# Gated linear attention with an MLP on one core: a new chunk order, uncast loads, and one queue for nearly every load

## The chip, the cores and the metric

The kernel runs on one core of a Trainium2 chip. The metric is the device time of one execution in microseconds (us). The fast executions of one kernel lie within 1.5% of each other here, often within 0.5%; an execution that is over 1.5% above the fastest of its kernel counts as slow and is left out of ratios. Times quoted for a kernel are medians over its runs. A ratio is computed as the mean time of one kernel's fast runs over the mean time of the other's fast runs of the same rounds on the same chip, so it is not quite the ratio of the medians that are quoted beside it. Experiments ran on several chips, so an experiment is judged by its ratio to the kernel before in its own rounds.

## The reference, cut to what matters

```python
# q, k, v, alpha: (B=4, H=8, S=768, D=48) float32
state = zeros((B, H, D, D))
for t in range(S):
    state = alpha[:, :, t, :, None] * state + einsum('bhd,bhe->bhde', k[:, :, t], v[:, :, t])
    y[:, :, t] = einsum('bhd,bhde->bhe', q[:, :, t], state)
x = y.transpose(0, 2, 1, 3).reshape(B * S, H * D)      # 3072 tokens x 384
h = maximum(x @ w_in, 0.0)                             # w_in 384 x 2048
out = (h * h) @ w_out                                  # w_out 2048 x 384
```

The recurrence carries a state from token to token within a batch. The four batches don't depend on each other.

## The kernel before

The kernel handles the sequence in 24 chunks of 128 tokens, six for each batch. Within a chunk it works with matrices: it takes the logarithm of alpha (L_s), sums it along the tokens with a matmul, forms A = exp(sum) and Ainv = exp(-sum), multiplies q by A and k by Ainv (qA and kI), transposes them, computes masked scores (sm), and adds the part that comes from the state of the chunk before (sb). The state (st) advances once in a chunk. The chunk's output, transposed into xT_big, is the input of the MLP. The MLP's matmuls need far more of TensorE than the recurrence, and a built-in planner weaves the two together.

It is a list scheduler that runs when the kernel is built. Every piece of work is an `Op` with an engine, an assumed duration and dependencies; the planner simulates the engines with those durations, and the kernel then emits every instruction in the planned order, which each engine keeps. If an assumed duration is wrong, the emitted program stays correct.

```python
class Plan:
    ...
    def run(self, gate):
        ...                      # picks, over all engines, the op that can start first (then by prio)
            op.start = t + getattr(op, "late", 0.0)
            free[eng] = t + op.dur
        ...
        self.order.sort(key=lambda o: o.start)     # instructions are emitted in this order
```

In the kernel before, the first four chunks of batch 0 are handled together. For these, alpha and q are loaded so that one partition takes four consecutive tokens. One descriptor row is then 4 x 48 floats, 768 bytes. All other q, k, v and alpha tiles have one token on a partition, so a row is 48 floats, 192 bytes. k and, later, alpha and q are issued by SyncE (seven of these transfers by GpSimd); v is cast to bf16 in its transfer, which GpSimd issues; the weights too are cast in their transfers by GpSimd.

```python
slot_srcs = {n: a[0, :, 0:4 * P, :].rearrange("h (p j) d -> p h (j d)", j=4) for n, a in srcs}  # 768-byte rows
srcs = [(n, a.rearrange("b h (c p) d -> b c p h d", p=P)) for n, a in srcs]                    # 192-byte rows
...
def pool_dma(dur, issue, emit, *deps):          # a transfer that GpSimd issues, in order
    i = add("POOL", issue, emit, *deps, *w_gate, prio=-50.0, lat=0.0, at=4.6)
    w_gate[:] = [i]
    return add("DMA", dur, lambda: None, i, lat=2.0)
...
def load_tile(nm):
    if nm == "vt":
        return loads.tile([P, H, D], BF16, name=nm, bufs=LBV)     # v: cast in the transfer
    return loads.tile([P, H, D], FP32, name=nm)
...
ld_at = [load_slots("at", i * H // 2, (i + 1) * H // 2) for i in range(2)]   # SyncE, 384 KB each
ld_qt = [load_slots("qt", i * H // 2, (i + 1) * H // 2) for i in range(2)]
for s in range(NJ):
    add_loads(s, ("kt", "vt"), pool=s == NJ - 1)
four_slots(ld_at, ld_qt)
...
for x in "iiiioo4oo5":                          # i, o: quarters of w_in, w_out (384 KB); 4, 5: a chunk's loads
    ...
```

Of the kernel before, what the change touches and what calls it, by code (L numbers as in the profile page):

```python
# [110 lines left out]
def kernel(  # L111
# [24 lines left out]
    slot_srcs = {n: a[0, :, 0:4 * P, :].rearrange("h (p j) d -> p h (j d)", j=4) for n, a in srcs}  # L136
    srcs = [(n, a.rearrange("b h (c p) d -> b c p h d", p=P)) for n, a in srcs]
# [7 lines left out]
    LBV = 6  # L145
# [10 lines left out]
    NJ = 4  # L156
    PQ = P // NJ
# [4 lines left out]
    kI_s = big.tile([P, NBUF, H, DP], BF16)  # L162
    ae_s = big.tile([P, NBUF, NP, 2], FP32)
    nc.vector.memset(warm, 0.0)
    for t in (L_s, qA_s, kI_s):
        nc.vector.memset(t[:, :, :, D:], 0.0)
    nc.vector.memset(ae_s, 0.0)
# [4 lines left out]

    t_lag = consts.tile([P, NJ, P], FP32)
    first_t = consts.tile([P, 1], FP32)
    mk4 = consts.tile([P, NJ, P], BF16)
    for c in range(NJ):
        nc.vector.memset(first_t[c * PQ:(c + 1) * PQ], -float(c * P))
    nc.gpsimd.iota(t_lag, pattern=[[-1, NJ], [1, P]], base=0, channel_multiplier=-NJ,
                   allow_small_or_imprecise_dtypes=True)
    nc.vector.tensor_scalar(mk4, t_lag, first_t, None, op0=ALU.is_ge)  # L180


    def within(out, cols, step=1):

        for base, sgn in ((0, 1), (PQ - 1, -1)):
            nc.gpsimd.affine_select(out=out, in_=out, compare_op=ALU.is_ge, fill=0.0,
                                    base=base, pattern=[[-PQ * sgn, NJ]] + cols, channel_multiplier=sgn)
    mq_incl = consts.tile([P, P], BF16)
    mq_strict = consts.tile([P, P], BF16)
    nc.gpsimd.memset(mq_incl, 1.0)  # L190
    within(mq_incl.rearrange("p (c u) -> p c u", c=NJ), [[0, PQ]])
    for out, base in ((mq_strict, -1), (mq_incl, 0)):
        nc.gpsimd.affine_select(out=out, in_=mq_incl, compare_op=ALU.is_ge, fill=0.0,
                                base=base, pattern=[[1, P]], channel_multiplier=-1)
    ones_blk = consts.tile([P, NJ], BF16)
    nc.gpsimd.memset(ones_blk, 1.0)
    within(ones_blk, [])

    def causal(out, pattern):
        nc.gpsimd.memset(out, 1.0)  # L200
        nc.gpsimd.affine_select(out=out, in_=out, compare_op=ALU.is_ge, fill=0.0,
                                base=0, pattern=pattern, channel_multiplier=-1)
    utri_p = consts.tile([P, 1, P], BF16)
    causal(utri_p[:, 0, :].rearrange("p (j t) -> p j t", j=NJ), [[1, NJ], [NJ, PQ]])
    ident_bf = consts.tile([P, P], BF16)
    make_identity(nc, ident_bf)
    utri_b = consts.tile([P, 1, P], BF16)
    causal(utri_b[:, 0, :], [[1, P]])
    ones_col = consts.tile([P, 1], BF16)
    nc.gpsimd.memset(ones_col, 1.0)  # L210
    slot = {n: big.tile([P, H, NJ, D], FP32, name=f"slot_{n}") for n in ("at", "qt")}
    qT4 = big.tile([P, NP, NJ, NJ, PQ], BF16)
    xT_big = big.tile([P, KT, n_tok], BF16)
    ident_by_token = ident_bf.rearrange("p (j t) -> p t j", j=NJ)
# [13 lines left out]
    def tr(*a):  # L228
# [4 lines left out]
        "sm0": -56.473, "cpq1": -50.279, "ps3": -49.423, "tq0": -43.954, "qA3": -43.948, "ln1": -42.551,  # L233
        "sb1": -40.005, "stm2": -40.004, "stm1": -40.000, "sb2": -40.000, "sb3": -40.000, "p13": -39.839,
        "kI1": -38.583, "p30": -36.979, "sb0": -36.132, "xT3": -35.894, "p31": -33.712, "sm1": -32.534,
        "pk": -31.000, "A0": -30.000, "pq0": -30.000, "qA0": -29.999, "Ai2": -29.995, "xn2": -29.992, "qA1":
        -29.899, "A1": -29.899, "pq1": -29.899, "qA2": -29.800, "pq2": -29.799, "xn1": -29.792, "A3":
        -29.700, "ps1": -28.550, "xn0": -27.270, "tq2": -22.798, "tq1": -22.219, "tq3": -20.369, "Ai0":
        -20.000, "A2": -19.910, "cp3": -19.910, "pq3": -19.909, "Ai1": -19.900, "Ai3": -19.699, "stm3":
        -19.005, "cpq2": -19.003, "pae": -19.000, "ae0": -18.999, "ln0": -17.727, "cp1": -17.717, "stm0":  # L240
        -17.111, "p10": -10.000, "cp0": -10.000, "kI0": -9.999, "p40": -9.999, "p21": -9.993, "p41": -9.989,
        "p32": -9.986, "p20": -9.984, "kI2": -9.980, "cp2": -9.980, "p11": -9.980, "ps2": -9.979, "p12":
        -9.979, "p43": -9.979, "p33": -9.970, "xn3": -9.970, "sm3": -9.970, "kI3": -9.969, "p23": -9.969,
        "p42": -9.960, "ps0": -9.272, "xT0": -9.000, "xT2": -9.000, "xT1": -9.000, "p22": -8.991, "ae1":
        -7.468, "cpq3": -6.554, "sm2": -6.554, "cpq0": -3.046,
# [15 lines left out]
    LD = 0.97  # L261
    WLD = 2.1
# [14 lines left out]
    X_ISSUE = 0.9  # L277
    w_gate = []

    def pool_dma(dur, issue, emit, *deps):  # L280

        i = add("POOL", issue, emit, *deps, *w_gate, prio=-50.0, lat=0.0, at=4.6)
        w_gate[:] = [i]
        return add("DMA", dur, lambda: None, i, lat=2.0)
# [16 lines left out]
    def hold_x(d, before, nm):  # L301
        def e_hold():
            d["at"] = loads.tile([P, H, D], FP32, name="at")
            pin(nc.gpsimd.tensor_copy(d["at"][:, 0, 0:1], before[nm][:, 0, 0:1]))
        d["go"] = add("POOL", 0.1, e_hold, before["ld_" + nm], prio=-6.0)

    PAIRS = 10
    C = [dict() for _ in range(NT)]
    state = {}
    made = {nm: [] for nm, _ in srcs}  # L310

    def load_tile(nm):
        if nm == "vt":
            return loads.tile([P, H, D], BF16, name=nm, bufs=LBV)
        return loads.tile([P, H, D], FP32, name=nm)

    def load_slots(nm, lo, hi):
        def ld():
            pin(nc.sync.dma_start(out=slot[nm][:, lo:hi].rearrange("p h j d -> p h (j d)"),  # L319
                                  in_=slot_srcs[nm][:, lo:hi]))  # L320
        return add("DMA", 2.5 * (hi - lo) / H, ld, lat=2.0, at=0.9)

    def add_loads(s, names=("at", "qt", "kt", "vt"), pool=False, after=None):
        d = C[s]
        b, c = divmod(s, NCH)
        for nm, src in srcs:
            if nm not in names:
                continue
            m = made[nm]
            n = LBV if nm == "vt" else LB  # L330
            prev = C[m[-n]]["use_" + nm] if len(m) >= n else None
            m.append(s)

            def ld(nm=nm, src=src):
                if nm not in d:
                    d[nm] = load_tile(nm)
                if nm == "vt" and after:
                    pin(nc.gpsimd.tensor_copy(d[nm][:, 0, 0:1], after["kt"][:, 0, 0:1]))  # L338
                pin((nc.gpsimd if pool or nm == "vt" else nc.sync).dma_start(out=d[nm], in_=src[b, c]))  # L339
# [514 lines left out]
```

## Time and profile before

| what | before | view |
|---|---|---|
| median of 3 runs | 192.5 us (191.35 to 194.46) | times |
| span of the profiled execution | 189.4 us | page |
| TensorE busy | 180.2 us, 95% | page |
| first w_in matmul | 22.50 us | chain of waits |
| quarters of w_in landed | 17.86, 20.34, 22.25, 24.15 us | GpSimd's waits |
| TensorE's granted clock | half from about 17.9 to 24.7 us | windows |

These lines are from the page of the kernel before: the span, the busy time of each engine, TensorE's granted clock in tenths and the transfer rate in 40 slices of the span, and the two DMA queues (packets, MB, share). PE is TensorE, POOL is GpSimd; q1 is the queue that SyncE issues to, q0 is GpSimd's.

```profile
span 189.4 us, 5215 instructions
...
PE 180.2 (95%) x1999; PEld 137.1 (72%) x1999; DVE 132.3 (70%) x335; ACT 126.7 (67%) x346; POOL 42.2 (22%) x78
...
PEclk9998589999999999999999999999999999999999
...
GB/s 177 238 165 203 204 223 211 125 183 147 183 191 185 206 180 173 201 153 188 218 130 142 166 84 124 170 87 126 0 45 43 3 42 45 6 37 45 42 42 83
...
q1 hardware_dynamic: 64992, 17.45, 44.8%
q0 software_dynamic: 29120, 6.88, 37.5%
```

TensorE is the bound for nearly the whole span. What can still be won lies in the first 22 us. The chain of waits that ended last (start us, length us, what) says what this start is made of:

```profile
6.33 9.01 DMA kt<-in_k_dram
...
22.50 15.27 PE bank L226 x139
...
167.36 18.95 PE bank L226 x152
```

A wait of 9 us for a k tile, then the state chain of the first chunks, and from 22.50 us on TensorE. The last of these lines is the final block of 152 matmuls.

The windows of the kernel before (window; busy us and instructions of PE, PEld, DVE, ACT, POOL; granted clock; DMA share; GB/s):

```profile
4.00:6.00 2.00, 1.54 (x13) 0.84 (x12) 0.00 (x0) 1.54 (x2) 1.99 (x5) 1.00 1.01 279
...
8.00:10.00 2.00, 2.00 (x22) 1.23 (x21) 0.57 (x2) 2.00 (x6) 2.00 (x4) 1.00 2.05 163
...
12.00:14.00 2.00, 1.23 (x20) 0.97 (x20) 1.23 (x3) 1.26 (x4) 0.77 (x1) 1.00 1.63 162
...
20.00:22.00 2.00, 2.00 (x25) 1.38 (x25) 1.73 (x4) 1.34 (x4) 0.88 (x1) 0.50 1.25 205
...
25.00:26.50 1.50, 1.50 (x22) 1.14 (x20) 0.51 (x2) 1.17 (x3) 0.38 (x1) 1.00 1.27 278
...
28.00:32.50 4.50, 4.50 (x44) 4.03 (x42) 2.95 (x8) 3.77 (x7) 2.66 (x3) 1.00 1.49 194
...
40.00:42.00 2.00, 2.00 (x25) 1.35 (x24) 1.29 (x2) 0.17 (x1) 0.00 (x0) 1.00 1.60 177
```

The last column is about 163 where k tiles in 192-byte rows and cast v tiles load together from the two queues (a cast tile counts with the 96 KB that it writes, not with the 192 KB that are read).

### The profile page before, as it was taken

The page shows a single profiled execution, that of the slowest core. Times are in us where ns is not written, and L with a number is a line of the kernel's source. Part 1 is how long each engine was busy: PE and PEld are TensorE (multiplying, and loading weights), DVE is VectorE, ACT ScalarE, POOL GpSimd, SP SyncE. Part 2 cuts the span into 40 slices and gives each one's busy share as a digit, 9 for nine tenths or more (in the row PEclk, how much of TensorE's full clock was granted, in tenths as well). Part 3 has the DMA queues.
Part 4 walks back from the last instruction along what each step waited for, and adds up shares of the span by engine and source line. Part 5 has one row for each costly group of instructions (what it writes and reads, how often), then busy time and mean ns, then how long its engine had stood idle before and what let it go on. Part 6 is the DMA issues. An engine that isn't in the chain of part 4 may idle for free.

```text
span 189.4 us, 5215 instructions
## 1 busy us (share of the span) xinstructions
PE 180.2 (95%) x1999; PEld 137.1 (72%) x1999; DVE 132.3 (70%) x335; ACT 126.7 (67%) x346; POOL 42.2 (22%) x78
## 2 busy tenths in 40 slices
PE   7864999999999999999999999999999999999993
PEld 2553778866878887777777787787787787777773
DVE  3167946754899795897886886886886886944411
ACT  3763459926778886678588588488588586565630
POOL 8967335023122233222021031041000000000000
PEclk9998589999999999999999999999999999999999
DMA  5999999899999999999959739739011011011112
GB/s 177 238 165 203 204 223 211 125 183 147 183 191 185 206 180 173 201 153 188 218 130 142 166 84 124 170 87 126 0 45 43 3 42 45 6 37 45 42 42 83
DMA packets 94280, 24.71 MB, mean 130 GB/s; under 512 B 85216, under 2 KB 93920, under 8 KB 94256
## 3 DMA queue, kind: packets, MB, share of 16 engines
q1 hardware_dynamic: 64992, 17.45, 44.8%
q0 software_dynamic: 29120, 6.88, 37.5%
q8 instruction: 15, 0.25, 0.6%
q14 instruction: 9, 0.07, 0.1%
q10 hardware_dynamic: 144, 0.05, 0.1%
HBM read 25.17 MB, written 4.72 MB: 158 GB/s over the span
## 4 chain that ended last, share of the span: by engine, by line
PE 87%; DMA 5%; SPq 3%; ACT 1%; DVE 1%; issue 1%; ACTq 0%; DVEq 0%
PE bank L226 78%; PE bank L229 7%; DMA kt<-in_k_dram 5%; PE st L226 2%; SPq L339 2%; SPq L319 1%; ACT r L668 1%; DVE st L578 1%; DVE sm L533 1%; ACT sb L583 0%; ACT xn L220 0%; DVE ob L736 0%; ACT ob L736 0%; ACT L_s L442 0%; DVE kI_s L474 0%
## 5 line engine op out<-in xcount | busy, mean ns | idle before, releaser
L668 ACT ACTIVATE r<-bank 128x256 bf16<-128x256 f32 (+1 forms) x160 | 64.7, 429 | 29.6 <-PE bank L226 28.2
L226 PE MATMUL bank<-xT_big,w_in_b 128*128 128x256 bf16 (+1 forms) x624 | 80.0, 266 | 0.1
L226 PE MATMUL bank<-w_out_b,gT 128*128 128x384 bf16 (+1 forms) x400 | 74.7, 320 | 0.0
L226 PEld LDWEIGHTS <-w_in_b 128*128 128x128 bf16 x624 | 53.8, 98 | 9.7 <-issue 0.5
L675 DVE TENSOR_TENSOR gT<-r 128x256 bf16<-128x256 bf16 (+1 forms) x160 | 47.6, 315 | 16.0 <-ACT r L668 14.4
L226 PEld LDWEIGHTS <-gT 128*128 128x128 bf16 x400 | 37.9, 98 | 15.8
L533 DVE TENSOR_TENSOR sm<-bank,utri_b 128x512 bf16<-128x512 f32 x40 | 25.3, 683 | 2.6 <-PE bank L226 2.5
L339 POOL DMA_DIRECT2D vt<-in_v_dram x24 | 21.3, 888 | 7.9 <-POOL vt L338 6.1
L338 POOL CAST vt<-kt 128x1 bf16<-128x1 f32 x18 | 4.7, 263 | 64.6 <-PE bank L226 41.8
L471 DVE TENSOR_TENSOR qA_s<-qt,A 128x384 bf16<-128x384 f32 x20 | 11.1, 556 | 9.5 <-ACT A L458 8.6
L218 DVE COPY qkT<-bank 128x1024 bf16<-128x1024 bf16 x20 | 13.8, 688 | 4.9 <-PE bank L229 4.9
L474 DVE TENSOR_TENSOR kI_s<-kt,Ainv 128x384 bf16<-128x384 f32 x24 | 13.3, 556 | 3.1 <-DMA kt<-in_k_dram 2.6
L709 ACT COPY ob<-bank 128x384 f32<-128x384 f32 x21 | 10.1, 480 | 8.1 <-PE bank L226 8.1
L226 PEld LDWEIGHTS <-qkT 64*128 64x128 bf16 (+1 forms) x260 | 10.4, 97 | 5.9 <-issue 2.5
L220 ACT CAST xn<-bank 128x384 bf16<-128x384 f32 x23 | 10.9, 480 | 4.2 <-PE bank L226 3.8
L583 ACT CAST sb<-st 128x384 bf16<-128x384 f32 x20 | 9.6, 478 | 5.7 <-DVE st L578 5.7
L458 ACT ACTIVATE A<-bank 128x384 bf16<-128x384 f32 x20 | 9.9, 496 | 2.4 <-PE bank L226 2.4
L229 PE MATMUL bank<-ident_bf,kI_s 128*128 128x128 bf16 x96 | 9.5, 223 | 2.1 <-DVE kI_s L474 2.1
L578 DVE TENSOR_TENSOR st<-st,ae_s 128x384 f32<-128x384 f32 x20 | 11.1, 556 | 0.0
L442 ACT ACTIVATE L_s<-at 128x384 bf16<-128x384 f32 x20 | 10.4, 521 | 0.0
L462 ACT ACTIVATE Ainv<-bank 128x384 bf16<-128x384 f32 x20 | 10.2, 510 | 0.0
L229 PE MATMUL bank<-ident_bf,qA_s 128*128 128x128 bf16 x96 | 9.3, 219 | 0.8 <-DVE qA_s L407 0.7
(78 smaller groups left out, 162.1 us busy)
## 6 DMA issues: line engine op xcount, KB each, us to landing
out_dram<-ob SPq DMA_DIRECT2D x23, 192.0 KB, 2.7
kt<-in_k_dram SPq DMA_DIRECT2D x21, 192.0 KB, 5.3
at<-in_alpha_dram SPq DMA_DIRECT2D x18, 192.0 KB, 4.8
qt<-in_q_dram SPq DMA_DIRECT2D x18, 192.0 KB, 4.7
vt<-in_v_dram POOLq DMA_DIRECT2D x24, 96.0 KB, 5.6
w_in_b<-in_moe_w_in_dram POOLq DMA_DIRECT2D x4, 384.0 KB, 11.0
w_out_b<-in_moe_w_out_dram POOLq DMA_DIRECT2D x4, 384.0 KB, 12.3
slot_at<-in_alpha_dram SPq DMA_DIRECT2D x2, 384.0 KB, 3.6
```

The lines of the kernel that those rows point to most:

```text
L218: pin(nc.vector.tensor_copy(out, in_))
L220: pin(nc.scalar.copy(out, in_))
L226: pin(nc.tensor.matmul(*a, **kw))
L229: pin(nc.tensor.transpose(*a))
L339: pin((nc.gpsimd if pool or nm == "vt" else nc.sync).dma_start(out=d[nm], in_=src[b, c]))
L442: pin(nc.scalar.activation(L[:, :, 0:D], d["at"], AF.Ln))
L471: pin(nc.vector.tensor_mul(qA[:, :, 0:D], d["qt"], d["A"]))
L474: pin((nc.vector if mk.eng == "DVE" else nc.gpsimd).tensor_mul(kI[:, :, 0:D], d["kt"], d["Ai"]))
L533: pin(nc.vector.tensor_mul(d["sm"][:, hh], d["sc"][hh], (utri_p if first else utri_b).to_broadcast([P, NP, P])))
L578: pin(nc.vector.tensor_mul(st4, st4, bcast(ae, D)))
L668: pin(nc.scalar.activation(box["r"], box["ph"], AF.Relu))
L675: pin(nc.vector.tensor_mul(gT[g][:, f0:f0 + nf, 0:n], box["r"], box["r"]))
```

## The change

The intent was to give the start independent work. The first chunks of the four batches don't wait for each other's state, so they are processed first, and then the rest batch by batch. The special code for the first four chunks of one batch goes. Every load but alpha of the first chunks of the first two batches is put on GpSimd's queue, in the order of need; the first chunks of two batches come in one transfer of 384 KB; v is no longer cast in its transfer but afterwards, by GpSimd (by ScalarE for first chunks, where the planner chooses).

The diff, cut to its core:

```diff
-    slot_srcs = {n: a[0, :, 0:4 * P, :].rearrange("h (p j) d -> p h (j d)", j=4) for n, a in srcs}
-    srcs = [(n, a.rearrange("b h (c p) d -> b c p h d", p=P)) for n, a in srcs]
+    srcs = {n: a.rearrange("b h (c p) d -> c p (b h) d", p=P) for n, a in srcs}
+
+    SEQ = [(b, 0) for b in range(B)] + [(b, c) for b in range(B) for c in range(1, NCH)]
 ...
     LD = 0.97
+    LDP = 1.15
+    LDS = 0.62
     WLD = 2.1
 ...
+    def load_pair(b, names):
+        for nm in names:
+            def ld(nm=nm):
+                t = loads.tile([P, 2, H, D], FP32, name=nm + "0", bufs=2)
+                pin(nc.gpsimd.dma_start(out=t.rearrange("p b h d -> p (b h) d"), in_=srcs[nm][0, :, b * H:(b + 2) * H]))
+                C[b][nm], C[b + 1][nm] = t[:, 0], t[:, 1]
+            C[b]["ld_" + nm] = C[b + 1]["ld_" + nm] = pool_dma(LDP, XP_ISSUE, ld)
 ...
+    def load(s, names=("at", "qt", "kt", "vt")):
+        b, c = SEQ[s]
+        for nm in names:
+            def ld(nm=nm):
+                C[s][nm] = loads.tile([P, H, D], FP32, name=nm)
+                pin(nc.gpsimd.dma_start(out=C[s][nm], in_=srcs[nm][c, :, b * H:(b + 1) * H]))
+            C[s]["ld_" + nm] = pool_dma(LDS, X_ISSUE, ld, C[s - LB]["use_" + nm] if s - LB >= B else None)
 ...
+        def e_vb():
+            d["vb"] = work.tile([P, H, D], BF16, name="vb0" if first else "vb", bufs=4)
+            if vb.eng == "POOL":
+                pin(nc.gpsimd.tensor_copy(d["vb"], d["vt"]))
+            else:
+                copy(vb, d["vb"], d["vt"])
+        vb = d["use_vt"] = add({"POOL": 0.52, "ACT": 0.37} if first else {"POOL": 0.52}, 0, e_vb, d["ld_vt"],
+                               C[s - 4].get("end") if s >= 8 else None, key=key("vb"), prio=-60.0)
 ...
-    ld_at = [load_slots("at", i * H // 2, (i + 1) * H // 2) for i in range(2)]
-    ld_qt = [load_slots("qt", i * H // 2, (i + 1) * H // 2) for i in range(2)]
-    for s in range(NJ):
-        add_loads(s, ("kt", "vt"), pool=s == NJ - 1)
-    four_slots(ld_at, ld_qt)
 ...
+    load_first("at")                              # alpha of batches 0 and 1, on SyncE
+    load_pair(0, ["qt"])
+    utri = add("POOL", 0.5, causal_mask, *w_gate, prio=-70.0)
+    load_pair(0, ["kt"])
+    ident = add("POOL", 0.5, identity, *w_gate, prio=-70.0)
+    load_pair(0, ["vt"])
+    load_pair(2, ["at", "qt", "kt", "vt"])
+    for s in range(4):
+        add_chunk(s)
+    order = ["i", "i", "i", "i", "o", "o", 4, "o", "o"]
+    for x in order + list(range(5, NT)):
 ...
```

## The prediction

> **What bounds the kernel now.** From 22.5 us on, TensorE. The page gives PE 180.2 of 189.4 us (95%), and the chain of waits that ended last is TensorE matmuls almost without a break from 22.50 to 186.3 us. Before that the chain is a load: 9.0 us of waiting for a kt transfer that ended at 15.34 us (released kI at 15.36), then the state recurrence of chunks 0 to 3 (st, sm, sb) up to 22.5 us, where the first w_in matmul starts (timeline). The windows show TensorE's granted clock at 0.50 from about 18 to 24.4 us, after TensorE was busy only 0.57 of 2 us in 14-16 us.
>
> **What the change does.**
> 1. Loads. v was cast in its transfer. With GpSimd's queue alone (24-36 us), uncast 192-byte-row loads move at 280-295 GB/s, so about 0.67 us per 192 KB (estimate); the stretch that ends with a cast vt load runs at 65-200 GB/s, so I put a cast vt at about 2 us of queue time (estimate: queue 0 is busy 37.5% of 189.4 us = 71 us; 8 weight loads at 1.95 us and seven plain loads leave about 2 us for each of 24 vt). In 8-15 us both queues run at 130-190 GB/s written. After: 16 unit loads (3.1 MB) in about 10.7 us from 2.3 us on: last first-chunk tile landed near 14 us, w_in from near 16 us (before: 17.9) to 22 us (before: 24.15).
> 2. Start-up work. No state chain among the first four chunks; the 32-row sums (0.83), the per-slot prefix matmuls (2.9 us) and the slow final transposes (about 0.81 us against 0.33 per chunk) go. ACT gets more: about 12.5 us of ln, exp, copies and two v casts before the last scores, from ln at 3.5 us; DVE about 9 us. Chaining these with the trace's durations (exp 0.51, multiply 0.556, mask 0.68, copy 0.38-0.59): first w_in matmul near 17 us, 5 us or so earlier.
> 3. Given back: of 20 state updates 19 instead of 16 fall into the dense part (+0.5 us); TensorE's half clock probably lasts to about 20-21 us, and the second pair of first chunks leaves about 1 us of gaps, as TensorE waits for their masks.
> 4. Steady part: unchanged work on TensorE. GpSimd issues 4 loads per chunk (0.89 us each) and casts v (about 0.5 us); it was 22% busy, so it keeps up. The Trainium skill ("SBUF — State Buffer", Who interferes with whom) says that DVE instructions with two SBUF inputs block, and are blocked by, GpSimd instructions that read SBUF: the 20 v casts against squares (0.29-0.42 us) and qA/kI. No run here shows it yet; DVE has some 20% slack, so I expect it to cost little.
>
> **On the critical path:** about 5 us of start, less 0.5 to 1 us: end 4 to 5 us earlier.
>
> **Predicted:** 187.8 us, 8 in 10 within 184.3 to 191.2. Chances: faster by over 2% 0.57, within 2% 0.39, slower 0.04.
>
> **What would show it.** First w_in matmul at 16-19 us in the timeline; no chain wait on kt after about 8 us; qt pair landed by 6 us, last vt by 15 us; the chain from about 20 us all TensorE; PEclk 0.5 ending before 22 us; dense stretch (first w_in matmul to last matmul) 163.8 us before, 164-166 after; GpSimd busy about 100 us, no long waits of TensorE for vb.
>
> **What would make it wrong.** 192-byte loads slower at the start than 280 GB/s, or GpSimd's descriptor writing slower for two-batch transfers; the start bound by ACT, so that the first w_in matmul stays at 19-20 us; half clock lasting longer; GpSimd's in-order queue holding a v cast behind a load that waits for a buffer; DVE delayed by the casts.

## More of the kernel before

`LDP` and `LDS` are what the planner assumes for a transfer of 384 KB and of 192 KB in 192-byte rows: 1.15 and 0.62 us, which is over 300 GB/s.

## The result, and the profile after

| what | before | after |
|---|---|---|
| median of 4 runs | 192.46 us (191.35 to 194.46) | 199.5 us (199.25 to 200.08) |
| ratio to the kernel before | 1 | 1.039, 95% interval 1.034 to 1.044 |
| span of the profiled execution | 189.4 us | 197.8 us |
| first w_in matmul | 22.50 us | 22.04 us |
| start of the final block of 152 matmuls | 167.36 us | 175.18 us |
| first w_in matmul to last matmul | 163.8 us | 172.1 us |
| GpSimd busy | 42.2 us | 97.2 us |

The change makes the kernel 3.9% slower. The prediction was 187.8 us, and its range ended at 191.2. Both profiled executions are fast ones. Of the kernel before, the execution of 194.46 us counts as slow, and the ratio leaves it out.

The same lines of the page, for the kernel after:

```profile
span 197.8 us, 5143 instructions
...
PE 183.4 (93%) x1973; PEld 138.6 (70%) x1973; DVE 132.4 (67%) x332; ACT 130.5 (66%) x359; POOL 97.2 (49%) x123
...
PEclk9955579966999999999999999999999999999999
...
GB/s 129 191 187 186 204 204 214 230 186 186 189 259 237 188 197 172 229 219 95 186 164 148 114 177 133 123 147 123 40 43 31 11 43 41 3 40 40 43 40 81
...
q0 software_dynamic: 9616, 21.63, 54.9%
q1 hardware_dynamic: 5680, 5.06, 8.1%
```

Two things are to be seen. The clock row has two stretches of half clock instead of one. And the second and third slice of the rate row (5 to 15 us), in which only tiles with 192-byte rows load, have 191 and 187 GB/s. The windows of the kernel after show it more finely, and show the second hole:

```profile
6.00:8.00 2.00, 1.82 (x18) 0.98 (x15) 0.10 (x1) 1.00 (x3) 2.00 (x3) 1.00 1.02 183
8.00:10.00 2.00, 0.79 (x8) 0.45 (x8) 1.53 (x4) 1.95 (x7) 2.00 (x3) 1.00 1.04 186
...
14.00:16.00 2.00, 1.65 (x26) 1.18 (x25) 0.72 (x2) 1.76 (x6) 0.79 (x2) 0.50 1.03 186
...
38.00:40.00 2.00, 0.72 (x10) 0.53 (x9) 0.69 (x1) 0.00 (x0) 0.96 (x2) 1.00 1.05 205
40.00:42.00 2.00, 0.00 (x0) 0.00 (x0) 0.00 (x0) 0.00 (x0) 1.74 (x3) 0.82 1.07 195
...
46.00:48.00 2.00, 2.00 (x14) 0.94 (x13) 0.99 (x2) 0.00 (x0) 1.79 (x3) 0.50 1.04 186
```

From 6 to 18 us the rate is 183 to 189 GB/s in every window. One pair transfer of 384 KB, 0.393 MB, then takes 2.1 us of the queue; the prediction had 1.34 us, and the planner 1.15. The pairs land 1.9 to 2.1 us apart (14.08, 16.00, 18.09, 20.07 us by GpSimd's waits). The first quarter of w_in follows: the first w_in matmul, which waits for it, starts at 22.04 us, and GpSimd's own wait for it ends at 22.28 us. In 40 to 42 us no compute engine but GpSimd does anything at all.

What GpSimd does then stands in the chain of waits of the kernel after:

```profile
12.83 14.87 DMA w_in_b<-in_moe_w_in_dram
...
27.99 11.65 DMA w_out_b<-in_moe_w_out_dram
...
39.92 0.88 POOL vt L306
...
40.91 0.88 POOL at L306
...
41.95 0.88 POOL qt L306
42.83 0.52 POOL vb L358
43.35 0.04 issue
43.40 0.48 PE st L189 x4
...
175.18 18.95 PE bank L189 x152
```

The lines of L306 are loads being issued, 0.88 us each; L358 is the cast of chunk 4's v. By GpSimd's waits in this trace, at most eight of its transfers are in flight: an issue first waits until the transfer eight places earlier has landed. So an issue waits for w_out to land, more issues follow, and the cast stands behind all of them in the same in-order program, although the v tile that it needs had landed by 36.03 us. TensorE waited for it, as the waits of the kernel after (engine, line, releaser: us in total, times, longest) say:

```profile
PE st L189 <- POOL vb L358: 4.7, 1, 4.7
```

Then TensorE, idle from 38.72 to 43.40 us, runs at half clock again until 48.10 us. The Trainium skill, "TensorE: Matmul & The Clock Gate", Part 1, says that the clock falls to half after an idle window of about 3.4 us and returns after about 3.4 us of sustained work; these windows run freely and do not start with the work. The trace has the same kind of fall and return: the clock falls at 41.27 us, 2.6 us after the work stopped, and returns 4.7 us after it resumed. At the start it is at half from 10.55 to 27.62 us, where TensorE was busy for 13.8 of 17.1 us, and it returns 5.6 us after the last pause (21.57 to 22.04 us). These four changes lie 5, 4 and 2 times 3.41 us apart, so in this trace the clock seems to be decided at the ends of stretches of 3.41 us (an inference from the four times).

A count of the MLP's matmuls in both traces dates the loss. By 38 us, the kernel before has done 96 w_in and 8 w_out matmuls, the kernel after 96 and 12: a tie. From 38 to 50 us, before does 15 and 48, after 0 and 22. The missing 15 and 26 are worth about 6.8 us (an estimate, with the page's busy time for one: 80.0 / 624 = 0.128 us and 74.7 / 400 = 0.187 us). The final block starts 7.82 us later. So the start gained nothing, and nearly all of the loss arises between 38 and 50 us.

### The profile page after: what moved, and what is told of

It is laid out like the page before. It is cut to its first block, busy times and chain, and to the rows that moved or that the text cites. A ratio compares the mean times of both kernels' runs of the same rounds, so it can differ in the third digit from the quotient of the medians.

```text
span 197.8 us, 5143 instructions
## 1 busy us (share of the span) xinstructions
PE 183.4 (93%) x1973; PEld 138.6 (70%) x1973; DVE 132.4 (67%) x332; ACT 130.5 (66%) x359; POOL 97.2 (49%) x123
## 3 DMA queue, kind: packets, MB, share of 16 engines
q0 software_dynamic: 9616, 21.63, 54.9%
## 4 chain that ended last, share of the span: by engine, by line
PE 76%; DMA 13%; POOL 7%; issue 1%; DVE 0%; ACT 0%; POOLq 0%
PE bank L189 68%; DMA w_in_b<-in_moe_w_in_dram 8%; PE bank L192 6%; DMA w_out_b<-in_moe_w_out_dram 6%; PE st L189 2%; POOL qt L286 1%; POOL kt L286 1%; POOL vt L286 1%; POOL w_in_b L253 1%; POOL at L286 1%; POOL qt L306 0%; POOL at L306 0%; POOL vt L306 0%; POOL vb L358 0%; POOL ident_bf L273 0%
## 5 line engine op out<-in xcount | busy, mean ns | idle before, releaser
L446 DVE TENSOR_TENSOR sm<-bank,utri_b 128x512 bf16<-128x512 f32 x48 | 30.4, 682 | 4.7 <-PE bank L189 4.6
L306 POOL DMA_DIRECT2D qt<-in_q_dram x20 | 17.7, 886 | 23.8 <-DVE gT L562 17.9
L389 DVE TENSOR_TENSOR qA_s<-qt,A 128x384 bf16<-128x384 f32 x24 | 13.6, 571 | 15.6 <-ACT A L376 14.6
L306 POOL DMA_DIRECT2D kt<-in_k_dram x20 | 17.7, 883 | 3.9 <-DMA w_in_b<-in_moe_w_in_dram 1.3
L306 POOL DMA_DIRECT2D at<-in_alpha_dram x20 | 17.7, 885 | 3.1 <-DMA kt<-in_k_dram 1.4
L358 POOL CAST vb<-vt 128x384 bf16<-128x384 f32 x20 | 12.2, 613 | 13.9 <-PE bank L189 12.5
L306 POOL DMA_DIRECT2D vt<-in_v_dram x20 | 17.7, 883 | 2.2 <-DMA w_in_b<-in_moe_w_in_dram 1.0
L181 DVE COPY qkT<-bank 128x1024 bf16<-128x1024 bf16 (+1 forms) x23 | 15.0, 650 | 5.2 <-PE bank L192 5.2
L365 ACT ACTIVATE L_s<-at 128x384 bf16<-128x384 f32 x24 | 12.4, 521 | 3.1 <-DMA at<-in_alpha_dram 3.1
L331 DVE TENSOR_TENSOR st<-st,ae_s 128x384 f32<-128x384 f32 x16 | 8.9, 555 | 4.5 <-PE st L189 4.5
## 6 DMA issues: line engine op xcount, KB each, us to landing
w_in_b<-in_moe_w_in_dram POOLq DMA_DIRECT2D x4, 384.0 KB, 13.1
```

The lines of the kernel that those rows point to most:

```text
L181: pin(nc.vector.tensor_copy(out, in_))
L306: pin(nc.gpsimd.dma_start(out=C[s][nm], in_=srcs[nm][c, :, b * H:(b + 1) * H]))
L358: pin(nc.gpsimd.tensor_copy(d["vb"], d["vt"]))
L365: pin(nc.scalar.activation(L[:, :, 0:D], d["at"], AF.Ln))
L389: pin(nc.vector.tensor_mul(qA[:, :, 0:D], d["qt"], d["A"]))
L446: pin(nc.vector.tensor_mul(d["sm"][:, hh], d["sc"][hh], utri_b.to_broadcast([P, NP, P])))
```

## The experiments

Three theories stood at the outset.

- **The queue theory** (Q): the loss is the 4.7-us wait and the half clock after it. GpSimd's in-order program holds the cast behind load issues. Move the cast, and the time returns to 192 to 194 us.
- **The load theory**: 192-byte rows load at about 187 GB/s, whatever is done. The first weights come late, so the start gains nothing; and the planner, which assumed 300 GB/s and more, put waits for data where there should have been work. The late cast is only the first of these waits.
- **The single-queue theory**: it is GpSimd's queue that is slow; with the loads on SyncE's queue as before, the rate returns.

Unless said otherwise, a diff is against the kernel after, and each run had three rounds against the kernel before (number 13 had five).

### 1. The casts of chunks 4 and 5 moved earlier on GpSimd, by 4 us of planned time

```diff
-        self.order.sort(key=lambda o: o.start)
+        self.order.sort(key=lambda o: o.start - getattr(o, "early", 0.0))
...
+        vb.early = {4: 4.0, 5: 4.0}.get(s, 0.0)
```

> Only change: on GpSimd the v casts of chunks 4 and 5 stand four places earlier in its instruction order, ahead of four load issues. Theory Q (queue order): the v data of chunk 4 had landed by 36.0 us, and its cast waited on GpSimd behind four load issues that each wait for the transfer eight places earlier to land; TensorE then idles 4.7 us (38.7 to 43.4) and runs at half clock to 48.2, which costs about 2.4 us more. Q expects the wait of TensorE for vb gone, no half clock after 28 us, and 192.3 to 193.8 us instead of 199.5. Rival D (data): the loads of this stage come too late, the cast's place does not matter: 198.5 to 200, with the cast still ending after 41 us. Rival S (steady part): the loss is spread over the dense part by casts against VectorE: about 199 too.

Measured: 198.03 us (197.88 to 198.78), ratio 1.032 (1.024 to 1.040). Chunk 4's cast now ran at 37.07 us, ahead of four load issues, and the wait of 4.7 us was gone. The time was not: by the medians, 1.5 us came back of the 7. The waits of this variant name the next in line, a wait of 2.1 us for a cast again and, on ScalarE, alpha that has not landed (4.5 us in 4 waits), and the chain has moved to that alpha:

```profile
PE st L189 <- POOL vb L358: 3.7, 2, 2.1
```

```profile
40.65 8.09 DMA at<-in_alpha_dram
```

The queue theory in its plain form falls: removing the longest wait uncovers late data.

### 2. The casts of chunks 4 to 7 on ScalarE

```diff
-            if vb.eng == "POOL":
+            if 4 <= s < 8:
+                pin(nc.scalar.copy(d["vb"], d["vt"]))
+            elif vb.eng == "POOL":
```

> Only change: the v casts of chunks 4 to 7 run on ScalarE instead of GpSimd; the load issues keep their order. Q expects the same as the cast moved up: 192.3 to 194 us, the ScalarE casts of about 0.5 us each costing little. D expects 198.5 to 200. Differs from the moved cast only if the casts themselves on GpSimd, not their place, cost time.

Measured: 199.65 us (199.47 to 199.99), ratio 1.040 (1.032 to 1.047): no gain at all. ScalarE's program is in order too, and the cast there waits for v to land (3.8 us in 3 waits). The chain shows 7.92 us of waiting for a v transfer from 44.07 us. This is again late data.

### 3. alpha, q and k of chunks 4 and on issued by SyncE

```diff
-                pin(nc.gpsimd.dma_start(out=C[s][nm], in_=srcs[nm][c, :, b * H:(b + 1) * H]))
+                pin((nc.gpsimd if nm == "vt" else nc.sync).dma_start(out=C[s][nm], in_=srcs[nm][c, :, b * H:(b + 1) * H]))
```

> Only change: alpha, q and k of chunks 4 to 23 are issued from SyncE's queue, v and the weights stay on GpSimd's. Q expects the v cast no longer stuck behind issues: wait for vb gone, 192 to 194 us. If what is slow is one queue for all loads, chunk 4's tiles also land beside the weights, some us earlier than 33 to 36 us, and w_out lands later than 29.9 and 39.9 us. D without Q: faster too, but by less than 3 us.

Measured: 201.27 us (200.97 to 201.69), ratio 1.048 (1.039 to 1.057): slower than the kernel after. The queue of the casts is empty of these issues, but SyncE starts them as early as buffers allow, and they then run beside the weights: the median time from issue to landing of a w_in quarter rises from 13.1 to 17.5 us, and the first w_in matmul starts at 25.6 us instead of 22.04.

### 4. The seven pair transfers issued by SyncE

```diff
-                pin(nc.gpsimd.dma_start(out=t.rearrange("p b h d -> p (b h) d"), in_=srcs[nm][0, :, b * H:(b + 2) * H]))
+                pin(nc.sync.dma_start(out=t.rearrange("p b h d -> p (b h) d"), in_=srcs[nm][0, :, b * H:(b + 2) * H]))
```

> Only change: the seven two-batch transfers of the first chunks are issued from SyncE's queue, so weights go to GpSimd's queue from about 3 us on. In the changed kernel the 192-byte rows moved at 169 to 201 GB/s from 6 to 18 us alone on GpSimd's queue, and w_in landed at 22.0 us. If that is what one queue of 192-byte rows gives, whoever makes the descriptors, then the two queues together exceed 200 GB/s written, w_in lands before 15 us and the first-chunk tiles later than before (last v after 20 us); first w_in matmul within 2 us of 22. If the descriptors of GpSimd were the limit, the first-chunk tiles land sooner than 18 us also beside the weights, and the first w_in matmul comes before 19 us. In both cases the vb wait near 40 us may shrink as GpSimd's queue runs ahead by seven issues: 190 to 196 us.

Measured: 228.18 us (227.25 to 231.11), ratio 1.187 (1.176 to 1.198). The profiled execution was a slow one, so only its ordering and rates are used here, not its length. The rate did not rise with the other queue: 187 GB/s in 2 to 6 us, 190 in 6 to 14, 199 in 14 to 30 and 186 in 30 to 50 us. From 48 to 54 us no data of GpSimd's queue are moving, and SyncE's queue alone, with 192-byte rows, makes no more than GpSimd's did in the kernel after:

```profile
48.00:54.00 6.00, 3.35 (x41) 2.51 (x40) 1.25 (x2) 4.16 (x12) 0.00 (x0) 0.50 1.38 186
```

So the rate is not a property of GpSimd's queue; the single-queue theory falls. The Trainium skill agrees: "DMA: Bandwidth & Descriptors", Issuing engines are not separate DMA queues, has all issuers share the same 16 engines. What changed is who gets the bandwidth. The pairs on SyncE's queue now compete with weights and later tiles on GpSimd's, and a k pair landed only at 55.0 us. The same page (Queues, rings and completion order) says that an engine takes turns between queues a packet at a time; a queue of short rows then gets a small share beside a queue of larger packets. The trace's records of single packets agree: from 10 to 14 us 625 packets of 1024 bytes completed on GpSimd's queue (weights) and 631 of 192 bytes on SyncE's, which is 160 against 30 GB/s.

### 5. First-chunk loads with the same bytes in long rows (wrong result)

The load theory's direct test. The first-chunk tiles take the same number of bytes into the same tiles, but from contiguous memory, so that a row has 1536 bytes (3072 in a pair) and not 192. The numbers that are loaded are the wrong tokens, so the result is wrong; the planner's constants and all other work are unchanged.

```diff
+    flats = {n: a.rearrange("b h s d -> (b h s d)").rearrange("(x p f) -> x p f", p=P, f=H * D) for n, a in srcs}
+    pairs = {n: a.rearrange("b h s d -> (b h s d)").rearrange("(x p f) -> x p f", p=P, f=2 * H * D) for n, a in srcs}
...
-                pin(nc.gpsimd.dma_start(out=t.rearrange("p b h d -> p (b h) d"), in_=srcs[nm][0, :, b * H:(b + 2) * H]))
+                pin(nc.gpsimd.dma_start(out=t.rearrange("p b h d -> p (b h d)"), in_=pairs[nm][b]))
...
-                pin(nc.sync.dma_start(out=C[s][nm], in_=srcs[nm][0, :, s * H:(s + 1) * H]))
+                pin(nc.sync.dma_start(out=C[s][nm].rearrange("p h d -> p (h d)"), in_=flats[nm][s]))
```

> Wrong result on purpose: the loads of the four first chunks read the same number of bytes as contiguous rows of 1536 or 3072 bytes instead of 192; nothing else changes. Theory R (row length): 192-byte rows move at about 187 GB/s whoever issues them (6 to 18 us here, and 180 to 210 GB/s in all with the pairs on SyncE too), rows of 768 bytes in the kernel before at 330 to 370 GB/s, and the 17 us of first-chunk loads push every later load back. R expects these loads done by about 11.5 us instead of 19, w_in landing near 14.5 us instead of 22.0, chunk 4 some 6 to 7 us sooner, and 190 to 193.5 us instead of 199.5; the cast stuck on GpSimd may still show, earlier. Rival Q (queue order alone): the wait for vb stays, 196 to 199 us.

Measured: 192.79 us (192.12 to 193.13), ratio 1.007 (1.004 to 1.011). The load rate doubles, as this window of the variant shows against 186 in the same window of the kernel after, and the first w_in matmul starts at 16.7 us, where the prediction had put it ("near 17 us"):

```profile
8.00:10.00 2.00, 1.26 (x14) 0.76 (x15) 1.98 (x5) 1.95 (x8) 1.15 (x2) 1.00 0.96 375
```

The later tiles still load in 192-byte rows, and the wait for the cast is still there:

```profile
PE st L191 <- POOL vb L360: 5.7, 1, 5.7
```

### 6. All q, k, v and alpha loads in long rows (wrong result)

```diff
  (the edit of experiment 5, and)
-                pin(nc.gpsimd.dma_start(out=C[s][nm], in_=srcs[nm][c, :, b * H:(b + 1) * H]))
+                pin(nc.gpsimd.dma_start(out=C[s][nm].rearrange("p h d -> p (h d)"), in_=flats[nm][b * NCH + c]))
```

> Wrong result on purpose: as the run with long rows in the first chunks, and the single loads of chunks 4 to 23 also read the same bytes as contiguous 1536-byte rows. With every load at over 300 GB/s the rate that the prediction assumed is given. If only that step was wrong, the rest of it holds: first w_in matmul at 16 to 18 us, no wait for vb, dense part as in the kernel before, 185.5 to 189 us. If GpSimd's order or its casts cost time by themselves, it stays at 190 us or more.

Measured: 188.06 us (187.32 to 188.87), ratio 0.983 (0.978 to 0.988). The page of this variant:

```profile
span 185.6 us, 5143 instructions
...
PEclk9999999999999999999999999999999999999999
...
GB/s 155 320 303 200 209 284 346 317 275 320 214 220 128 164 157 126 148 182 134 156 172 100 158 170 110 147 133 42 42 4 44 45 1 48 42 0 46 42 42 87
```

The order, the casts on GpSimd and the arithmetic are those of the kernel after; the loads alone differ, and the time is 188.06 us against a prediction of 187.8. First w_in matmul to last matmul takes 166.2 us (15.77 to 181.94), at the edge of the predicted 164 to 166. So the rest of the prediction, that the independent chunks make the start earlier by some 5 us and that less is given back, holds in its direction once the loads are fast. That the sum fits to 0.3 us is partly luck: the loads were faster than assumed (295 to 359 GB/s in the windows from 4 to 12 us, not 280 to 295), the start gained 6.7 us and not 5, and the dense stretch grew by 2.4 us (163.8 to 166.2) and not by 0.5 to 1. One long wait for a cast is left as well:

```profile
PE st L191 <- POOL vb L360: 2.6, 1, 2.6
```

One caution belongs here: an issue of long rows also takes GpSimd less time (0.53 us against 0.88, GpSimd busy 64.0 us), so that this run shortens loads and issues together. Experiment 14 will keep the issues long (about 0.9 us).

### 7. The kernel before with its four slot loads split into 192-byte rows

The counterpart: take the long rows from the kernel before, with a right result. The diff is against the kernel before.

```diff
-            pin(nc.sync.dma_start(out=slot[nm][:, lo:hi].rearrange("p h j d -> p h (j d)"),
-                                  in_=slot_srcs[nm][:, lo:hi]))
+            for j in range(4):
+                pin(nc.sync.dma_start(out=slot[nm][:, lo:hi, j, :],
+                                      in_=slot_srcs[nm][:, lo:hi, j * D:(j + 1) * D]))
```

> The kernel before, right result, with its four slot loads (768-byte rows) cut into sixteen of 192-byte rows; all else as before. R expects 1.57 MB at about 187 instead of 330 to 370 GB/s: alpha, q and the k tiles behind them 3.5 to 4 us later, first w_in matmul at about 26 us, 195 to 197 us. If row length does not matter, 191 to 193 us.

Measured: 211.47 us (210.69 to 212.18), ratio 1.104 (1.099 to 1.109). The direction is as the load theory has it, and the rate falls from 279 to 180 GB/s in this window:

```profile
4.00:6.00 2.00, 1.72 (x14) 0.88 (x12) 0.00 (x0) 0.62 (x1) 1.99 (x5) 1.00 0.98 180
```

The size is some four times what was expected (20 us instead of 4 to 6), and the chain tells why:

```profile
12.61 21.55 DMA kt<-in_k_dram
34.18 0.57 DVE kI_s L475
```

Sixteen issues in place of four keep SyncE busy until 11 us, so the k tiles are issued 8 us later, and they then run beside the weights of the other queue and land at 34.18 us. This run is therefore in keeping with the load theory, but it does not show what the 768-byte rows are worth: the additional issues and the contention are in it.

### 8. v cast in its transfer again

```diff
-                t = loads.tile([P, 2, H, D], FP32, name=nm + "0", bufs=2)
+                t = loads.tile([P, 2, H, D], BF16 if nm == "vt" else FP32, name=nm + "0", bufs=2)
...
-                C[s][nm] = loads.tile([P, H, D], FP32, name=nm)
+                C[s][nm] = (loads.tile([P, H, D], BF16, name=nm, bufs=8) if nm == "vt"
+                            else loads.tile([P, H, D], FP32, name=nm))
...
-            d["vb"] = work.tile([P, H, D], BF16, name="vb0" if first else "vb", bufs=4)
-            if vb.eng == "POOL":
-                pin(nc.gpsimd.tensor_copy(d["vb"], d["vt"]))
-            else:
-                copy(vb, d["vb"], d["vt"])
+            d["vb"] = d["vt"]
```

> The changed kernel with v cast to bf16 in its transfer again, as before, so no v casts on GpSimd or ScalarE. My prediction put a cast v load at about 2 us of queue time against 0.67 uncast. If the number of 192-byte rows sets the time, a cast v takes the same 1.05 us as an uncast one: w_in lands within 1 us of 22.0, and as no cast is stuck on GpSimd the time is that of the run with the cast moved up, 197 to 199 us. If a cast load is slower, by 1 us each, the start moves back by 4 us: 202 us or more.

Measured: 194.4 us (194.1 to 194.59), ratio 1.016 (1.014 to 1.018), against 197 to 199 expected. The planned order is unchanged. The prediction had assumed that a cast v tile takes about 2 us of the queue and an uncast one 0.67. GpSimd's timeline shows the opposite. Its waits for the k pair and then the v pair of batches 2 and 3 end where the next issues start; first the kernel after, then this variant:

```profile
18.09 0.90 POOL L306 DMA_DIRECT2D at<-in_alpha_dram  x1 [1.35 <-DMA kt<-in_k_dram]
20.07 0.89 POOL L306 DMA_DIRECT2D qt<-in_q_dram  x1 [1.08 <-DMA vt<-in_v_dram]
```

```profile
17.41 0.90 POOL L307 DMA_DIRECT2D at<-in_alpha_dram  x1 [1.43 <-DMA kt<-in_k_dram]
18.68 0.89 POOL L307 DMA_DIRECT2D qt<-in_q_dram  x1 [0.38 <-DMA vt<-in_v_dram]
```

From k's landing to v's: 1.98 us uncast, 1.27 us cast, for the same 384 KB read. The cast makes the transfer shorter. It also takes the v cast out of GpSimd's program, so that this run alone does not say how much is due to which.

### 9. The same loads, the order made anew with measured durations

```diff
-    LDP = 1.15
-    LDS = 0.62
-    WLD = 2.1
+    LDP = 2.1
+    LDS = 1.05
+    WLD = 1.95
...
-        i = add("POOL", issue, emit, *deps, *w_gate, prio=-50.0, lat=0.0, at=0.8)
+        i = add("POOL", issue, emit, *deps, *w_gate, *flight[-8:-7], prio=-50.0, lat=0.0, at=0.8)
         w_gate[:] = [i]
-        return add("DMA", dur, lambda: None, i, lat=2.0)
+        flight.append(add("DMA", dur, lambda: None, i, lat=2.0))
+        return flight[-1]
```

The planner now knows the measured length of a load, and that no more than eight transfers are in flight.

> The changed kernel, its static order made anew with the measured durations in place of the assumed ones (a two-batch load 2.1 instead of 1.15 us, a single load 1.05 instead of 0.62, a weight load 1.95 instead of 2.1) and with at most eight GpSimd transfers in flight. The same loads in the same order. If the loss is that the order was made for loads that are too fast, a good part returns: no wait for vb over 1 us, 194 to 197 us; the start (first w_in matmul near 22 us) stays. If the late data cost this much in any order: 198 us or more.

Measured: 192.24 us (192.15 to 193.6), ratio 1.006 (1.000 to 1.013). The loads are as slow as before (first w_in matmul at 21.86 us), and the loss is gone: first w_in matmul to last matmul takes 165.1 us, and no long wait for a cast is left. This separates two terms. Slow loads cost the gain at the start; an order made for fast loads costs some 7 us on top as long as the loads are slow. The final block starts at 167.97 us, against 175.18 in the kernel after:

```profile
167.97 18.95 PE bank L189 x152
```

### 10. Experiment 9 with v cast in its transfer

```diff
  (experiments 8 and 9 together, and the cast's op leaves the plan; the planner is told 1.4 us for a cast pair and 0.7 us for a cast tile)
```

> As the new order with measured durations, and v cast in its transfer again (0.7 us for a single one), no v cast on any engine. The run with v cast in its transfer alone gave 194.4 us with TensorE waiting several times for data between 38 and 56 us. Expected 191 to 193.5 us: a tie with the kernel before, because the 192-byte rows of alpha, q and k remain.

Measured: 190.37 us (190.04 to 191.92), ratio 0.997 (0.990 to 1.003): the same as the kernel before, within what three rounds resolve.

### 11. The kernel before with w_in held back until k of chunk 2 has landed (a miss)

The thought was that the kernel before could have its 9-us wait for k shortened by keeping the weights out of the way. The diff is against the kernel before.

```diff
+        first = ready is w_in_ready and not ready
...
+            if first:
+                pin(nc.gpsimd.tensor_copy(dst[:, 0, 0:1], C[2]["kt"][:, 0, 0:1]))
...
-        ready.append([pool_dma(WLD, W_ISSUE, e_issue)])
+        ready.append([pool_dma(WLD, W_ISSUE, e_issue, C[2]["ld_kt"] if first else None)])
```

> A try at beating both: the kernel before, with its first weight transfer held back on GpSimd until the k tile of chunk 2 has landed, so that the k tiles do not share the DMA engines with the weights. With short slot rows the k tiles fell behind the weights and landed at 34 us, so the sharing matters. Expected: k of chunk 2 lands near 13 us instead of 15.3, first w_in matmul 1 to 2 us sooner than 22.5, w_in from about 17 us, 190 to 191.5 us against 192 of the kernel before. If the later loads are what limits, no gain or a loss of up to 1 us.

Measured: 192.38 us (191.68 to 193.23), ratio 1.007 (1.000 to 1.014). k still landed at about 15.2 us, and the DMA queues then ran dry: 28 GB/s in 14 to 16 us and 6 in 16 to 18 us. Weights were not what delayed that tile.

### 12. Experiment 10 with the recurrence allowed less lead over the MLP (a miss, with a freak)

```diff
-    LEAD = 4
+    LEAD = 3
```

> As the new order with v cast in its transfer, and the attention chunks let run three instead of four tiles ahead of the MLP, so that TensorE's order puts less work that waits for loads before MLP work that is ready. If waits for data between 38 and 56 us are left, 0.5 to 2 us better than the same with four; if not, equal within 0.5 us or a little worse.

Measured: 205.23 us by the median, ratio 1.070 (1.063 to 1.078). The diff is against experiment 10. Three runs took 203.89 to 205.26 us; the profiled one took 631.15 us, with TensorE 99% busy at a recorded clock of 1.0. The 1.0 is no measurement: the page of this execution has no clock row. In it, w_in matmuls of 128x256 took 692 ns on average, against 278 in the kernel after, where none of those up to 60 us, at half clock too, took over 418. TensorE itself was thus slower than at half clock, for a reason that is not shown. There is no usable profile of this variant, and neither its slowness in the other three runs nor the freak execution is explained.

### 13. Experiment 10 with q and k cast in their transfers as well

The diff is against experiment 10; the planner is told the durations of cast loads for q and k too.

```diff
-                t = loads.tile([P, 2, H, D], BF16 if nm == "vt" else FP32, name=nm + "0", bufs=2)
+                t = loads.tile([P, 2, H, D], BF16 if nm != "at" else FP32, name=nm + "0", bufs=2)
...
-                C[s][nm] = (loads.tile([P, H, D], BF16, name=nm, bufs=8) if nm == "vt"
+                C[s][nm] = (loads.tile([P, H, D], BF16, name=nm, bufs=8 if nm == "vt" else LB) if nm != "at"
```

> The new order with measured durations, and q, k and v all cast to bf16 in their transfers (alpha stays in float). In the run with v cast a cast pair took about 1.4 us of queue time against 2.1 uncast. If time per load is what holds the start, the first-chunk loads take 12.6 instead of 16.8 us, w_in lands near 18 us, first w_in matmul at 17 to 19 us, and 186 to 188.5 us: better than both kernels by 2% or more. If what is left is in the order or on the other engines, 189.5 to 191 as with v alone. The error may grow a little from the rounding of q and k.

Measured: 187.84 us over six runs (186.99 to 189.74), ratio 0.983 (0.976 to 0.990). The result is correct within the reference's tolerance. The first w_in matmul starts at 17.9 us, and the stretch from there to the last matmul is 164.5 us. This is the lowest time of a correct version. It beats the kernel before by 1.75%; the interval, 1.05% to 2.45%, rules out that there is no gain but leaves open whether the gain is over 2%.

### 14. The kernel after, its order untouched, with q, k and v cast in their transfers

```diff
  (the edit of experiment 8, with nm != "at" in place of nm == "vt"; the planner's constants are those of the kernel after)
```

> The changed kernel in its old order, with q, k and v cast in their transfers and no v casts on engines. If slow loads alone are the cause and the old order fits loads that are fast enough, 188 to 191 us. If the order is a cause of its own, 192 us or more, near the 194.4 us of v cast alone.

Measured: 189.05 us (188.94 to 189.25), ratio 0.987 (0.981 to 0.993). The first w_in matmul starts at 18.93 us. The planner still assumes the fast loads of the change, and the issues still take 0.93 to 0.96 us each on average. Compared with experiment 8, only q's and k's casts in the transfer are added, no planned order moves, and the ratio falls from 1.016 to 0.987. Two things get shorter: the loads, and VectorE's multiplications of q and k, which now read bf16 (358 ns against 557). The runs don't separate them, but the first w_in matmul still waits for its weights (0.54 us), so it is the loads that set the start. Together with experiment 6, where the casts on GpSimd and float multiplications stayed, this shows that the loads' time is the main term. The time of experiments 13 and 14 can't be told apart (their intervals overlap): with short loads the old order is nearly as good as the new.

The queue line of this variant's page holds a surprise, against `9616` packets and `54.9%` in the kernel after:

```profile
q0 software_dynamic: 79888, 14.56, 96.4%
```

Eight times the packets and a larger booked share of the engines, and yet the data land sooner. Neither the packet count nor the share on the page is a measure of how long a load takes.

### 15 and 16. The two halves of experiment 9, one at a time

Experiment 9 changed two things in the planner. Number 15 keeps the measured durations but not the limit of eight transfers in flight; number 16 keeps the limit but the old durations.

```diff
  (15: of experiment 9 only LDP, LDS and WLD)
```

> The changed kernel in an order made with the measured load durations, without the limit of eight GpSimd transfers in flight. Same loads, casts on GpSimd. With both the time was 192.2 us. If the durations are what mattered, 191.5 to 194 us. If the limit mattered, casts are again stuck behind load issues, 196 us or more.

```diff
  (16: of experiment 9 only *flight[-8:-7] and the list behind it)
```

> The changed kernel in an order made with the old, too short load durations, but with the limit of eight transfers in flight. If the limit mattered, 192 to 195 us. If the durations did, TensorE's order again puts chunk work ahead of its data, 196 to 199 us.

Measured: 209.14 us (208.45 to 209.61), ratio 1.092, for the durations alone, and 199.54 us (199.39 to 199.94), ratio 1.042, for the limit alone. The waits of number 15, and a line of the chain of number 16:

```profile
PE st L189 <- POOL vb L359: 12.7, 1, 12.7
```

```profile
40.94 8.03 DMA at<-in_alpha_dram
```

With true durations but no limit, the planner puts even more issues ahead of the cast, and these wait for landings that the planner doesn't know of: the cast of chunk 4 runs at 51.48 us, behind twelve issues, although its tile had landed by 36.49 us. With the limit but false durations, the casts come on time (from 35.9 us, waiting only for v to land), and TensorE is still held up by alpha that lands late. Each half alone helps nothing; the order is good only when the planner knows both.

## Why the prediction was wrong, point by point

**The step that failed** is the first term of point 1: "uncast 192-byte-row loads move at 280-295 GB/s, so about 0.67 us per 192 KB (estimate)". The trace of the change shows 183 to 189 GB/s, about 1.05 us for 192 KB. The 280 to 295 were read in windows of 1 to 1.5 us just behind a weight transfer (278 in 25 to 26.5 us, 293 in 32.5 to 33.5 us), and the windows beside them have 203, 194 and 164. In these windows the last packets of the weights and the first of the tiles behind them complete side by side. By the trace's records of single packets, one of 4224 bytes (as much as 22 rows) took 176 ns by the median from 25.5 to 26 us, but 364 ns from 27.5 to 28 us, and 373 ns in the kernel after from 6 to 16 us. The prediction took the highest short window for the sustained rate, although its own text had "130-190 GB/s" for 8 to 15 us and put that down to two queues sharing.

**The second term of the same sum was wrong in sign.** "I put a cast vt at about 2 us of queue time" was inferred from the booked share of queue 0. Experiment 8 measures 1.27 us for a pair that is cast, 0.64 us for 192 KB, against 1.98 us for a pair that is not. The prediction charged the kernel before for the cast and credited the change for dropping it; dropping it made v's loads longer.

**What followed from this.** "w_in from near 16 us" became 22.28 us; "first w_in matmul near 17 us, 5 us or so earlier" became 22.04 us, 0.46 us earlier. The change also gave up the only fast loads of the kernel before: alpha and q of four chunks, 1.57 MB, came in 768-byte rows. At 187 instead of about 285 GB/s (279 to 296 in the three windows from 2 to 8 us) these cost about 2.9 us more (an estimate from the two measured rates: 8.4 against 5.5 us). The prediction did not count that.

**What the prediction named as a risk and priced too low.** "GpSimd's in-order queue holding a v cast behind a load that waits for a buffer" happened, with the landing of the eighth transfer before in place of a buffer, 4.7 us in the trace. "192-byte loads slower at the start than 280 GB/s" happened too. But slower for 2% or more had a chance of 0.04, because the two were thought of as small and separate. They are one: the order was planned for the fast loads, so slow loads turned into waits of in-order engines. Experiment 9 prices it: with the same slow loads, a new order recovers the loss (ratio 1.039 to 1.006).

**What was right.** TensorE bounds the kernel before and experiment 6 for nearly all of the time from the first w_in matmul on. With fast loads (experiment 6) the time is 188.06 us and w_in matmuls start at 15.8 us, so point 2, the saving at the start, holds in its direction. Its size and the price of point 3 were both too low (6.7 us and 2.4 us); that they nearly cancel is luck. GpSimd's busy time, "about 100 us", was 97.2. "I expect it to cost little", of the v casts against VectorE, held: the Trainium skill ("SBUF — State Buffer", Who interferes with whom) says that a VectorE instruction with two inputs in SBUF and a GpSimd instruction that reads SBUF block each other. The trace has v casts of 0.52 us as a rule and up to 1.11 us, and VectorE's squares at 324 ns on average against 315 before; VectorE's total is 132.4 us against 132.3.

**What stays open.** Why a cast in the transfer shortens a load in 192-byte rows is not shown by any run. How much of experiment 7's loss is the rows and how much its additional issues is not separated, nor how much of experiments 13 and 14 is VectorE's shorter multiplications. And experiment 12 has no explanation.

## What to carry to other kernels

Before moving loads about, read the rate that each kind of row sustains over several microseconds when it is alone in flight, and check it against landing times; a peak in a short window next to another kind of transfer is no rate. A layout that gives long rows (here 768 bytes) may be the best thing in a kernel, so price what a change gives up, not only what it removes. Where a static planner fixes the order of in-order engines, its assumed load times and its limit on transfers in flight are part of the kernel: an order made for loads that are 1.7 to 1.8 times too fast cost more here than the slow loads themselves, and correcting only one of the two did not help.

## What the Trainium skill lacked or had wrong

- "DMA: Bandwidth & Descriptors", Specifications, says that transfers below 512 bytes don't reach line rate, and its section Why small descriptors are slow gives an overhead of about three cycles beside one beat for each 32 bytes. For 192 bytes that is 6 of 9 cycles, two thirds; of the page's limit of about 358 GB/s that makes some 239 GB/s (an estimate from the page). The runs have 183 to 189 GB/s for 192-byte rows, 344 to 375 for rows of 1536 to 3072 bytes (in three of the four 2-us windows from 4 to 12 us of experiment 5; the fourth has 243). The direction agrees, and the rate is lower than the estimate. That estimate holds for rows that start on a 256-byte boundary, as one in four of these does; for others the page (How a descriptor splits into AXI transactions) adds beats, which are left out here, so the runs do not show the page wrong. It has no measured figure for rows this short on this chip.
- No page that I read says what a cast in the transfer does to load time. With 192-byte rows, a pair of 384 KB took 1.27 us from landing to landing when cast to bf16 against 1.98 us uncast.
- "DMA: Bandwidth & Descriptors", Anatomy of one DMA, fits a transfer of GpSimd's as 2.0 us plus bytes over 436 GB/s, 2.9 us for 384 KB. As the time of one transfer alone this was not tested here; as a spacing in a full queue it doesn't apply: pairs landed 1.9 to 2.1 us apart, set by their rows.
- The same page, Queues, rings and completion order, has the turns between queues, but no figure for what a queue of short rows gets beside a queue of weights. Experiment 4 has one: 30 of 190 GB/s, at equal numbers of packets. A k pair then landed only at 55.0 us, and in experiment 7, with the same two kinds of queue, k at 34.18 us.
- "TensorE: Matmul & The Clock Gate", Part 1, speaks of an idle window of about 3.4 us. The window need not be idle: the kernel after fell to half clock at 10.55 us, after 3.41 us in which TensorE was busy for 1.94 us and paused for 0.70 us at most. The page has no figure for the share of busy time that decides. These runs give no single one: the clock fell after a stretch of 3.41 us with 2.26 us busy (experiment 13, at 14.93 us) and did not fall after one with 1.55 us (experiment 1, at 46.20 us, counted in steps of 3.41 us from the changes of its clock), unless matmul records are missing there.
